# Seven block products of the last layer in another order, with other places for their operands and sums

## The chip, the cores and the metric

The kernel runs on one core of one Trainium2 chip. The metric is device time in microseconds. The kernel before takes 352.95 us (median of 3 runs, 352.54 to 353.83).

Engines are named as in the profile: PE (TensorE, matmuls), ACT (ScalarE), DVE (VectorE), POOL (GpSimdE), SP (SyncE, which issues the DMAs). PE writes into PSUM, which has eight banks here; ACT and DVE read the banks out. Each engine runs its instructions in the order of the program and waits where an operand is not there yet, so everything behind a waiting instruction waits too.

## The reference

Local attention over 4 batches, 8 heads and 576 positions, then a soft mixture of 8 experts, then a gated layer. Only the last layer matters here:

```
# x: 2304 tokens x 512, w_in: 512 x 2048, w_out: 2048 x 512, float32
h = x @ w_in
g = h * (1.0 / (1.0 + np.exp(-h)))      # SiLU
return g @ w_out
```

## The kernel before

**What is computed where.** The mixture's 32 slot outputs times `w_in` are kept as `astk` (tile `rv_astk`), and the mixture's weights of all tokens as `ct`, so a block of h is one matmul. The layer's second product `g @ w_out` is done in two ways. The first 768 tokens go through plain products: for each of 16 slices f of the hidden size, operations `h0.f` (matmul), `si0.f` and `gh0.f` (ACT, SiLU in float32 and rounded), `gl0.f` (DVE, the rounding's rest) and `om0.t.f` (three matmuls of 512 columns for each of six token blocks t). `oe0.t` reads the six sums out of the banks.

The other 1536 tokens are done in two rounds c = 0, 1 of 768 tokens, and here the product is cut into 2 x 2 blocks and done with seven block products in place of eight (Strassen's scheme in Winograd's form). The four activation blocks are A, B, C and E (two halves of the tokens, even and odd slices f), each of eight tiles of 128 x 384. Their operations:

- `ch` is the matmul for one tile into bank 6 or 7 in turn, `cs` the SiLU that ACT writes from it to the block's place (L1051). A `ch` needs the `cs` of two tiles earlier to have freed its bank.
- `sx` are sums of blocks on DVE (L1013, or L1016 where two tiles don't lie side by side): B := A - B, D := C - B, A := A + D, D := E - D. Before, D has a place of its own, `x`, the tile that held the plain part's activations.
- `sh` (ACT, L1068) rounds two tiles of a block for one product into a ring of three (`rs_sth`), and `sl` (DVE, L1070) writes the rest (`rt_stl`).
- `pp` is PE's part: twelve matmuls of 384 columns for two tiles; a product has 48 of them. The weights are plain blocks (tiles `ws`) or sums of weight blocks (`t2.*`, `t34.*`, and halves of `ws`), made by `ts` (sums, DVE L715, L717, L719), `th` (rounded, ACT L723) and `tl` (rest, DVE L728).
- `pe` reads banks out: copies on ACT (L1093), adds on DVE (L1097, L1100). `do` stores a piece of the output.

**Places.** SBUF places are reused under other names: place `w15` holds the last weights in float32 (`wt3`), which `ts`, `th` and `tl` of the weight slices 6 and 7 read, and then block E (`raww15`). `w7` holds `wt2`, then the last sums `t34.3`. A new tile in a place can be written when the last reader of the old one is done; the table `FREE` and the lists `place` tell the planner which operations these are.

**What sets the order.** `list_schedule` walks a table of estimated costs, dependencies and priorities, and fixes each engine's order ahead of the launch. What it is not told of it can't plan around: the wait is then there on the chip all the same, and everything behind it in that engine's order stands.

Of the kernel before, what the change touches and what calls it, by code (L numbers as in the profile page):

```python
# [32 lines left out]
def fused_kernel(ctx: ExitStack, tc: tile.TileContext, a: dict):  # L33
# [784 lines left out]
    for f in (0, 1, *range(2, 16, 2)):  # L818
        i = f // 2
# [5 lines left out]
    for i in range(8):  # L825
# [5 lines left out]
                 3: [["cvi3.0"], [f"t{x}{j}.{k}" for j in (2 * (i // 2) - 2, 2 * (i // 2) - 1) for k in (1, 3) for x in "hl"]][i > 1],  # L831
# [59 lines left out]
    def ost(i):  # L891
        return (hsb, lgf, vz, ccf)[i][:, 0:512] if i < 4 else rawt("x")[:, 2048 + 512 * (i - 4):2560 + 512 * (i - 4)]
# [139 lines left out]
    for c in range(NC):  # L1032
        prev = c - 1
        todo = [(b, i) for b in "ABCE" for i in range(8)]
        for b, i in todo:
# [3 lines left out]
            x = f"{c}.{'ABCDE'.index(b)}.{i}"  # L1039
# [3 lines left out]
            if b == "E":  # L1043
                d = ([f"{q}{c}.2.{i//2-2}" for q in ("sh", "sl")] + [f"sx{c}.4.{i//2-2}"] if i >= 4 else
                     [f"{q}{prev}.2.{i//2+2}" for q in ("sh", "sl")] + [f"sx{prev}.4.{i//2+2}"] if c else FREE["w15"])
            elif c:
# [394 lines left out]
```

## Time and profile before

| | before |
|---|---|
| median of 3 runs | 352.95 us |
| the profiled execution | 352.64 us |
| its span, first to last instruction | 350.5 us |
| PE busy | 333.1 us, 95% |
| DVE busy | 264.9 us, 76% |
| ACT busy | 217.8 us, 62% |
| from the last DVE add's start to the end of the span | 3.7 us |

The times in the trace are microseconds from the start of the span. The seven products of round 0 begin at 214.3, and from there on PE has only these products and their `ch` matmuls left, with a few of the plain part in between. The last DVE add starts at 346.77. A row of the timeline gives start, duration, engine, line, operation, tiles, count, and in brackets the engine's idle time before it with what ended it. Matmuls overlap: one of 384 columns lasts 0.33 from start to end, but the next starts 0.17 later.

### The profile page before, as it was taken

To read this page: it belongs to the slowest core of one execution; us is meant where nothing else is said; L and a number is where in the kernel's file an instruction comes from. 1 tells how busy PE (TensorE), PEld (TensorE's weight loads), DVE (VectorE), ACT (ScalarE), POOL (GpSimd) and SP (SyncE) were. 2 spreads that over 40 slices of the span, in tenths; PEclk is the share of its full clock that TensorE was granted. 3 is DMA by queue.
4 is the path that set the end of the run, shared out by engine and by line. 5 is a ranking of instruction groups with operands and counts; after the bars stand their busy time and mean duration, and the time that the engine had idled before them with its cause. 6 is when DMAs were issued, how large, how long until landed. Compare 5 with 4: busy or idle time off the path is not lost.

```text
span 350.5 us, 8136 instructions
## 1 busy us (share of the span) xinstructions
PE 333.1 (95%) x3200; PEld 270.9 (77%) x3211; DVE 264.9 (76%) x478; ACT 217.8 (62%) x623; POOL 74.4 (21%) x121
## 2 busy tenths in 40 slices
PE   7999999998999998999999999969999999999995
PEld 3687877876533336778767879949999999999995
DVE  5778778699620389999999999969755689965651
ACT  2699989886240136687584999765545677644430
POOL 6987978575430000000000000000000000000000
PEclk9999999999999999999999999999999999999999
DMA  7999999999999998645560003100101110001111
GB/s 262 403 406 404 409 396 407 415 412 413 421 415 424 410 417 340 243 179 197 185 280 2 0 0 122 60 0 2 45 1 47 45 47 0 0 3 45 47 45 45
DMA packets 17893, 70.03 MB, mean 200 GB/s; under 512 B 1984, under 2 KB 4288, under 8 KB 12096
## 3 DMA queue, kind: packets, MB, share of 16 engines
q1 hardware_dynamic: 17856, 69.53, 50.3%
q8 instruction: 25, 0.41, 0.5%
q14 instruction: 12, 0.10, 0.1%
HBM read 64.80 MB, written 4.72 MB: 198 GB/s over the span
## 4 chain that ended last, share of the span: by engine, by line
PE 53%; DVE 20%; ACT 10%; DMA 8%; issue 4%; POOL 3%; SPq 1%; ACTq 0%; POOLq 0%; DVEq 0%
PE ps L86 50%; DMA w_wi<-in_w_in 3%; DMA w_wo<-in_w_out 3%; PE ps L312 2%; ACT rt_px L232 2%; DVE x_gz L876 2%; ACT rv_astk L774 2%; DVE rt_stl L1070 2%; DMA rs_raw<-in_v 2%; DVE w_wif L634 1%; POOL rt_px L249 1%; DVE w_wif L632 1%; ACT rt_gtm L867 1%; DVE w_ws L693 1%; DVE w_wt L632 1%
## 5 line engine op out<-in xcount | busy, mean ns | idle before, releaser
L1068 ACT CAST rs_sth<-w_raww 128x768 fp32r<-128x768 f32 (+1 forms) x44 | 34.3, 779 | 34.5 <-PE ps L86 31.6
L1070 DVE TENSOR_TENSOR rt_stl<-w_raww,rs_sth 128x768 fp32r<-128x768 f32 (+1 forms) x44 | 38.6, 882 | 20.3 <-ACT rs_sth L1068 20.3
L86 PE MATMUL ps<-w_ws,x_gz 128*128 128x512 f32 x216 | 53.2, 393 | 0.0
L86 PE MATMUL ps<-rs_sth,w_ws 128*128 128x384 f32 x192 | 51.7, 334 | 0.0
L232 ACT ACTIVATE rt_px<-ps,spaced 128x64 f32<-128x64 f32 x144 | 43.7, 334 | 10.3 <-DVE spaced L228 9.4
L86 PEld LDWEIGHTS ps<-w_ws,x_gz 128*128 128x128 f32 x216 | 40.0, 188 | 8.2 <-DVE x_gz L876 0.7
L86 PEld LDWEIGHTS ps<-rs_sth,w_ws 128*128 128x128 f32 x192 | 34.9, 188 | 0.0
L1051 ACT ACTIVATE w_raww<-ps 128x384 f32<-128x384 f32 x64 | 28.8, 491 | 8.0 <-DVE ra_t2.1_2528 L728 3.3
L86 PE MATMUL ps<-ct_ct,rv_astk 128*128 128x384 f32 x96 | 27.5, 350 | 5.5 <-ACT w_raww L1051 2.4
L232 ACT ACTIVATION_READ_ACCUMULATOR rt_px<-ps,spaced 128x1 f32 x144 | 32.5, 226 | 0.0
L86 PE MATMUL ps<-rt_stl,w_ws 128*128 128x384 f32 x96 | 32.1, 334 | 0.0
L86 PEld LDWEIGHTS ps<-ct_ct,rv_astk 128*128 128x128 f32 x96 | 17.1, 188 | 11.1 <-ACT x_gz L873 4.5
L1070 DVE TENSOR_TENSOR rt_stl<-x_rawx,rs_sth 128x768 fp32r<-128x768 f32 x16 | 15.3, 956 | 11.6 <-ACT rs_sth L1068 11.6
L249 POOL TENSOR_TENSOR rt_px<-rt_px,stats 128x576 f32<-128x576 f32 (+2 forms) x17 | 18.6, 1092 | 8.3 <-DVE stats L245 2.3
L1068 ACT CAST rs_sth<-x_rawx 128x768 fp32r<-128x768 f32 x16 | 13.4, 836 | 9.3 <-PE ps L86 9.1
L86 PEld LDWEIGHTS ps<-rt_stl,w_ws 128*128 128x128 f32 x96 | 18.0, 188 | 0.0
L867 ACT ACTIVATE rt_gtm<-ps 128x768 f32<-128x768 f32 (+1 forms) x17 | 13.2, 775 | 5.3 <-PE ps L86 4.0
L876 DVE TENSOR_TENSOR x_gz<-rt_gtm,x_gz 128x768 fp32r<-128x768 f32 (+1 forms) x17 | 15.4, 906 | 0.5 <-ACT x_gz L873 0.2
L86 PEld LDWEIGHTS ps<-ra_a,rv_v 128*64 128x64 f32 x320 | 13.1, 137 | 2.8 <-DVE ra_a L263 1.1
L86 PE MATMUL ps<-ra_a,rv_v 128*64 128x96 f32 (+2 forms) x320 | 14.6, 241 | 0.5 <-DVE ra_a L263 0.3
L86 PE MATMUL ps<-rb_a,rv_v 128*64 128x96 f32 (+2 forms) x320 | 14.5, 241 | 0.1
L86 PEld LDWEIGHTS ps<-rb_a,rv_v 128*64 128x64 f32 x320 | 13.1, 137 | 1.9 <-issue 1.1
(293 smaller groups left out, 757.1 us busy)
## 6 DMA issues: line engine op xcount, KB each, us to landing
w_wi<-in_w_in SPq DMA_DIRECT2D x7, 1024.0 KB, 7.7
rs_wo<-in_w_out SPq DMA_DIRECT2D x4, 1024.0 KB, 5.8
rk_k<-in_k SPq DMA_DIRECT2D x12, 288.0 KB, 7.7
w_wo<-in_w_out SPq DMA_DIRECT2D x3, 1024.0 KB, 4.8
rs_raw<-in_v SPq DMA_DIRECT2D x9, 288.0 KB, 8.8
rs_raw<-in_q SPq DMA_DIRECT2D x8, 288.0 KB, 6.7
w_more<-in_q SPq DMA_DIRECT2D x8, 288.0 KB, 10.0
w_more<-in_v SPq DMA_DIRECT2D x6, 288.0 KB, 8.2
```

The source lines that it names most:

```text
L86: pe.matmul(out, lhsT=lhsT, rhs=rhs, start=start, stop=stop, skip_group_check=True)
L232: act.activation(out=preg(n)[:, j, :], in_=sj(n, j), func=ACTF.Exp, scale=D ** -0.5, bias=nmx[:, r, j // 3, j % 3:j % 3 + 1], accum_out=su ...
L249: pool.tensor_tensor(out=p, in0=p, in1=rinv[:, n % 2, j0:j1].rearrange("p (j o) -> p j o", o=1).to_broadcast([128, j1 - j0, 64]), op=ALU.mult)
L312: pe.transpose(ps[0:m, c:c + 128], x[:, 128 * t:128 * t + m], ident)
L632: dve.scalar_tensor_tensor(out=out, in0=hi, scalar=0xC0000000, in1=out, op0=ALU.bitwise_and, op1=ALU.bitwise_or)
L634: dve.scalar_tensor_tensor(out=out, in0=lo, scalar=29, in1=out, op0=ALU.logical_shift_right, op1=ALU.bitwise_or)
L774: act.copy(out=asl(f)[32 * r:32 * r + 32], in_=(aqh if r < 2 else aql)[rows])
L867: act.activation(out=cols(gt(f), ss), in_=hbs(ss), func=ACTF.Silu)
L876: dve.tensor_tensor(out=gsl(gbuf(f, 1), ss), in0=gsl(gt(f), ss), in1=gsl(gbuf(f, 0), ss), op=ALU.subtract)
L1051: op(f"cs{x}", "ACT", .42, [f"ch{x}", *d], lambda c=c, b=b, i=i, s=s: act.activation(out=at(c, b, i), in_=bank[6 + s][:, 0:TW], func=ACTF. ...
L1068: op(f"sh{x}", "ACT", cost(c, PRODS[p][0], j, .42, .74), [*src, old, "cvo14" if o < 0 else None], lambda c=c, p=p, j=j: both(c, p, j, 0, l ...
L1070: lambda c=c, p=p, j=j: both(c, p, j, 1, lambda x, h, l: dve.tensor_tensor(out=l, in0=x, in1=h, op=ALU.subtract)))
```

## The change

- **Order of the products** (table `PRODS` and `SEQ`). Before: A, D = C - B, E, B, A, C, D in the order of the table. Now the products are run in the order A, E, C (all plain), then C := C - B, A := A + C, B := A - B and E := E - C.
- **Places.** There is no block D: sums overwrite C and E. `ROOMS` and `ROOM` deal blocks A, E, C, B of round 0 to the places w8 and w12, w11 and w10, w13 (and ends of four others), and `x`. Block B therefore waits for the plain part's last matmul. Place w15 holds only a bank's copy, V.
- **Banks and read-outs.** The first product of a bank pair starts it, and later ones add to it or start it anew. The read-outs are nine steps instead of seven, with eight more ACT copies in all.
- **Dependencies told to the planner.** `th{i}.3` and place w15 now also name the parts `.2` of `tl`.
- **The last product.** Its last two weight slices run for bank 5 first and then for bank 4.
- One plain read-out (`oe0.4`) goes to the end of place w13.

```diff
-                 3: [["cvi3.0"], [f"t{x}{j}.{k}" for j in (2 * (i // 2) - 2, 2 * (i // 2) - 1) for k in (1, 3) for x in "hl"]][i > 1],
+                 3: [["cvi3.0"], [f"t{x}{j}.{k}" for j in (2 * (i // 2) - 2, 2 * (i // 2) - 1) for k in (1, 2, 3) for x in "hl"]][i > 1],
...
-            "w15": [f"tl{i}.{k}" for i in (6, 7) for k in (1, 3)]}
...
+            "w15": [f"tl{i}.{k}" for i in (6, 7) for k in (1, 2, 3)]}
+    ROOMS = ([(p, n) for p in ("w8", "w12") for n in range(4)], [(p, n) for p in ("w11", "w10") for n in range(4)],
+             [("w13", n) for n in range(4)] + [(p, 4) for p in ("w8", "w12", "w11", "w10")], [("x", n) for n in range(8)])
+    ROOM = ("AECB", "EBAC")
...
-    PRODS = (("A", 0, 0), ("D", 1, 2), ("E", 0, 5), ("B", 1, 3), ("A", 2, 1), ("C", 1, 4), ("D", 2, 6))
+    PRODS = (("A", 0, 0), ("C", 0, 2), ("E", 1, 5), ("B", 0, 3), ("A", 1, 1), ("C", 2, 4), ("E", 2, 6))
+    SEQ = (0, 2, 5, 1, 4, 3, 6)
...
+        end = (c, p) == (NC - 1, SEQ[-1]) and i > 5
+        for x, m in ((6, i - 6), (7, i - 6)) if end else ((i, 0), (i, 1)):
...
+            op(f"sx{c}.3.{j}", "DVE", cost(c, "AB", j, .476, .88), r("A") + r("B"), lambda c=c, j=j: csum(c, "B", "A", "B", ALU.subtract, j))
+            op(f"sx{c}.2.{j}", "DVE", cost(c, "CB", j, .476, .88), [f"sx{c}.3.{j}", *r("C"), *st(5)], lambda c=c, j=j: csum(c, "C", "C", "B", ALU.subtract, j))
+            op(f"sx{c}.1.{j}", "DVE", cost(c, "AC", j, .476, .88), [f"sx{c}.2.{j}", *st(0)], lambda c=c, j=j: csum(c, "A", "C", "A", ALU.add, j))
+            op(f"sx{c}.4.{j}", "DVE", cost(c, "EC", j, .476, .88), [f"sx{c}.2.{j}", *r("E"), *st(2)], lambda c=c, j=j: csum(c, "E", "E", "C", ALU.subtract, j))
...
+        X, Y, Z = range(3)
+        for k, p, b, o in ((0, 0, (X,), "T"), (2, 2, (Y, "T"), "T"), (5, 5, (Z,), "V"), (1, 1, (X,), "U"), (4, 4, (Y, "U"), "U"), (8, 4, (Y,), "W"), (3, 3, (X, "V"), "V"), (9, 3, (X, "W"), "W"), (6, 6, (Z, "U"), "U")):
```

In the order of the instructions, three places show what moved.

ACT, where block E's first SiLUs stand. Before, E is `w15_raww15`, written from `ps_81` (PSUM) behind the two casts of the last weight sums `t34.3`, which read `wt3`:

```order
L1051 ACTIVATE w11_raww11_2605<-ps_81 128x384
L723 CAST w7_t34.3_2725<-w15_wt3_2324 128x512
L1051 ACTIVATE w10_raww10_2642<-ps_81 128x384
L723 CAST w7_t34.3_2725<-w15_wt3_2324 128x512
L1093 COPY vz_65<-ps_81 128x384
L1093 COPY cc_68<-ps_81 128x384
L1051 ACTIVATE w15_raww15_2752<-ps_81 128x384 x2
L1068 CAST rs_sth_2546<-x_rawx_2676 128x768
```

Now E is `w11_raww11` and `w10_raww10`, and the same casts stand among E's SiLUs:

```order
L1037 ACTIVATE w11_raww11_2601<-ps_81 128x384 x2
L723 CAST ra_t2.1_2526<-w7_wt2_2189 128x256
L723 CAST ra_t2.1_2526<-w15_wt3_2324 128x256
L1052 CAST rs_sth_2545<-w11_raww11_2601 128x768
L1037 ACTIVATE w10_raww10_2652<-ps_81 128x384 x2
L723 CAST w7_t34.3_2662<-w15_wt3_2324 128x512 x2
L1052 CAST rs_sth_2545<-w11_raww11_2601 128x768
L1037 ACTIVATE w10_raww10_2652<-ps_81 128x384 x2
```

E has left place w15, and no SiLU of a block stands behind the last reader of `wt3` any more.

DVE, around the last weight parts (L728). Before, the sums D (`x_rawx`, L1013 and L1016) stand ahead of the last one, which reads `wt3`, and the casts' rests (`rt_stl`) behind it:

```order
L1070 TENSOR_TENSOR rt_stl_2557<-x_rawx_2676,rs_sth_2546 128x768
L719 TENSOR_TENSOR w15_wt3_2324<-w15_wt3_2324 128x256
L728 TENSOR_TENSOR ra_t2.1_2528<-w7_wt2_2189,ra_t2.1_2528 128x256
L728 TENSOR_TENSOR w7_t34.3_2725<-w15_wt3_2324,w7_t34.3_2725 128x512 x2
L728 TENSOR_TENSOR w4_ws6_2363<-w15_wt3_2324,w4_ws6_2363 128x256
L728 TENSOR_TENSOR w5_ws7_2439<-w15_wt3_2324,w5_ws7_2439 128x256
L728 TENSOR_TENSOR ra_t2.1_2528<-w15_wt3_2324,ra_t2.1_2528 128x256
L1016 TENSOR_TENSOR x_rawx_2676<-w8_raww8_2538,w10_raww10_2642 128x384
L1016 TENSOR_TENSOR x_rawx_2676<-w12_raww12_2573,w10_raww10_2642 128x384
L1016 TENSOR_TENSOR x_rawx_2676<-w11_raww11_2605,w10_raww10_2642 128x384
L1016 TENSOR_TENSOR x_rawx_2676<-w10_raww10_2642 128x384
L728 TENSOR_TENSOR ra_t2.1_2528<-w15_wt3_2324,ra_t2.1_2528 128x256
```

Now all weight parts are through before the first sum (L1001), and the sums begin behind `oe0.5` (L928):

```order
L728 TENSOR_TENSOR ra_t2.1_2526<-w15_wt3_2324,ra_t2.1_2526 128x256
L728 TENSOR_TENSOR w4_ws6_2363<-w15_wt3_2324,w4_ws6_2363 128x256
L728 TENSOR_TENSOR w5_ws7_2439<-w15_wt3_2324,w5_ws7_2439 128x256
L1054 TENSOR_TENSOR rt_stl_2555<-w10_raww10_2652,rs_sth_2545 128x768 x2
L1054 TENSOR_TENSOR rt_stl_2555<-w13_raww13_2694,rs_sth_2545 128x768 x2
L928 COPY x_rawx_2781<-ps_81 128x512
L1001 TENSOR_TENSOR x_rawx_2781<-w8_raww8_2536,x_rawx_2781 128x768
L1001 TENSOR_TENSOR w13_raww13_2694<-w13_raww13_2694,x_rawx_2781 128x768
```

Eight block sums that stood among the weight parts have moved behind them.

PE, around the plain part's last three matmuls, `om0.5.15` (`w5_ws7,x_gz`). Before, they stand between two steps of the first product:

```order
L86 MATMUL ps_81<-ct_ct_1667,rv_astk_1933 128x384 x2
L86 MATMUL ps_81<-w5_ws7_2439,x_gz_1940 128x512 x3
L86 MATMUL ps_81<-ct_ct_1667,rv_astk_1933 128x384
L86 MATMUL ps_81<-rs_sth_2546,w2_ws4_2251 128x384
L86 MATMUL ps_81<-rt_stl_2557,w2_ws4_2251 128x384
```

Now they stand ahead of the last step of the second product, and the `ch` of two tiles of B (`ct_ct,rv_astk`) behind that step:

```order
L86 MATMUL ps_81<-w5_ws7_2439,x_gz_1940 128x512 x3
L86 MATMUL ps_81<-rs_sth_2545,w5_ws7_2439 128x384
L86 MATMUL ps_81<-rt_stl_2555,w5_ws7_2439 128x384
L86 MATMUL ps_81<-rs_sth_2545,w5_ws7_2439 128x384 x2
L86 MATMUL ps_81<-rt_stl_2555,w5_ws7_2439 128x384
L86 MATMUL ps_81<-rs_sth_2545,w5_ws7_2439 128x384
L86 MATMUL ps_81<-ct_ct_1667,rv_astk_1933 128x384 x2
```

The plain part's end has moved back by more than a whole product, and place `x`, now block B's, comes free that much later.

## Rows read from the trace of the kernel before

**Rows 1.** The page: busy time of PE, and its granted clock by slices.

```profile
PE 333.1 (95%) x3200; PEld 270.9 (77%) x3211; DVE 264.9 (76%) x478; ACT 217.8 (62%) x623; POOL 74.4 (21%) x121
...
PEclk9999999999999999999999999999999999999999
```

**Rows 2.** Windows: stretch, busy us (count) of PE, PEld, DVE, ACT, POOL, clock, DMA.

```profile
207.59:226.53 18.94, 18.94 (x100) 17.52 (x100) 18.91 (x32) 18.10 (x40) 0.00 (x0) 1.00 0.22 84
226.53:241.14 14.61, 11.37 (x58) 9.79 (x58) 11.89 (x20) 7.91 (x17) 0.00 (x0) 1.00 0.00 0
241.14:346.73 105.59, 105.59 (x609) 105.27 (x608) 71.34 (x93) 54.65 (x90) 0.00 (x0) 1.00 0.08 27
```

**Rows 3.** Timeline of PE from 227 to 237, where it waits.

```profile
227.74 0.34 PE L86 MATMUL ps<-ct_ct,rv_astk 128*128 128x384 f32 x1
229.00 0.44 PE L86 MATMUL ps<-ct_ct,rv_astk 128*128 128x384 f32 x1 [0.91 <-ACT w_raww L1051]
...
232.22 0.34 PE L86 MATMUL ps<-rs_sth,w_t2.0_1877 128*128 128x384 f32 x1
234.05 0.82 PE L86 MATMUL ps<-ct_ct,rv_astk 128*128 128x384 f32 x2 [1.49 <-ACT w_raww L1051]
235.15 0.44 PE L86 MATMUL ps<-rs_sth,ra_t2.1_2528 128*128 128x384 f32 x1 [0.28 <-ACT rs_sth L1068]
236.15 0.44 PE L86 MATMUL ps<-rt_stl,ra_t2.1_2528 128*128 128x384 f32 x1 [0.55 <-DVE rt_stl L1070]
```

**Rows 4.** Timeline of ACT in the same stretch.

```profile
227.94 0.62 ACT L723 CAST w_t34.3_2725<-w_wt 128x512 fp32r<-128x512 f32 x1 [1.34 <-DVE ra_t2.1_2528 L728]
228.46 0.48 ACT L1051 ACTIVATE w_raww<-ps 128x384 f32<-128x384 f32 x1
...
229.35 0.48 ACT L1093 COPY vz<-ps 128x384 f32<-128x384 f32 x1
...
233.51 0.87 ACT L1051 ACTIVATE w_raww<-ps 128x384 f32<-128x384 f32 x2 [3.29 <-DVE ra_t2.1_2528 L728]
```

**Rows 5.** Timeline of DVE from 217 to 235.

```profile
217.01 1.82 DVE L1013 TENSOR_TENSOR w_raww<-w_raww,w_raww 128x768 f32<-128x768 f32 x2
...
222.30 0.68 DVE L928 COPY x_rawx<-ps 128x512 f32<-128x512 f32 x1
...
227.43 0.41 DVE L728 TENSOR_TENSOR ra_t2.1_2528<-w_wt,ra_t2.1_2528 128x256 fp32r<-128x256 f32 x1
...
231.10 1.49 DVE L1016 TENSOR_TENSOR x_rawx<-w_raww,w_raww 128x384 f32<-128x384 f32 x3
...
232.98 0.42 DVE L728 TENSOR_TENSOR ra_t2.1_2528<-w_wt,ra_t2.1_2528 128x256 fp32r<-128x256 f32 x1
235.13 0.96 DVE L1070 TENSOR_TENSOR rt_stl<-x_rawx,rs_sth 128x768 fp32r<-128x768 f32 x1 [1.74 <-ACT rs_sth L1068]
```

**Rows 6.** Timeline of PE and of ACT around 207, where the plain part's last SiLU ends.

```profile
200.24 4.26 PE L86 MATMUL ps<-w_ws,x_gz 128*128 128x512 f32 x18
204.34 0.51 PE L86 MATMUL ps<-ct_ct,rv_astk 128*128 128x384 f32 x2
204.68 2.22 PE L86 MATMUL ps<-w_ws,x_gz 128*128 128x512 f32 x9
207.14 0.61 PE L86 MATMUL ps<-ct_ct,rv_astk 128*128 128x384 f32 x2 [0.24 <-ACT x_gz L873]
...
205.27 0.41 ACT L723 CAST w_ws<-w_wt 128x256 fp32r<-128x256 f32 x1
205.58 0.81 ACT L867 ACTIVATE rt_gtm<-ps 128x768 f32<-128x768 f32 x1
```

**Rows 7.** Timeline of the last matmul and the last two adds.

```profile
346.24 0.56 DVE L1100 TENSOR_TENSOR hsb<-ps,hsb 128x384 f32<-128x384 f32 x1 [3.89 <-PE ps L86]
346.39 0.34 PE L86 MATMUL ps<-rs_sth,w_ws 128*128 128x384 f32 x1
346.77 0.56 DVE L1100 TENSOR_TENSOR lg<-ps,lg 128x384 f32<-128x384 f32 x1
```

More of the change, by code (lines that the diff above doesn't have):

```diff
@@ L1033, in fused_kernel @@
         prev = c - 1
-        todo = [(b, i) for b in "ABCE" for i in range(8)]
+        todo = [(b, i) for b in "AECB" for i in range(8)]
         for b, i in todo:
@@ L1042, in fused_kernel @@
             hist.append(f"ch{x}")
[L1043 to L1046, printed above, removed]
-                p = {"A": 3, "B": 4, "C": 5}[b]
-                d = [f"{q}{prev}.{p}.{i//2}" for q in ("sh", "sl")]
-            else:
-                d = FREE[home[b, i][0]]
+            if c:
+                p, more = {"A": (1, (1, 4)), "E": (4, ()), "C": (3, ()), "B": (6, ())}[b]
+                d = [f"{q}{prev}.{p}.{i//2}" for q in ("sh", "sl")] + [f"sx{prev}.{k}.{i//2}" for k in more]
+            else:
+                o, n = place(c, b, i)
+                d = FREE[o] + (["do5"] if o == "x" and n > 6 else [])
@@ new lines, in fused_kernel @@
+                op(f"pp{c}.{p}.{i}", "PE", 6 * .172, d, lambda c=c, p=p, i=i: pmm(c, p, i))
+        X, Y, Z = range(3)
+        for k, p, b, o in ((0, 0, (X,), "T"), (2, 2, (Y, "T"), "T"), (5, 5, (Z,), "V"), (1, 1, (X,), "U"), (4, 4, (Y, "U"), "U"), (8, 4, (Y,), "W"), (3, 3, (X, "V"), "V"), (9, 3, (X, "W"), "W"), (6, 6, (Z, "U"), "U")):
+            for m in range(2):
+                last_ = (c, p) == (NC - 1, SEQ[-1])
+                d = [f"pp{c}.{p}.{6 if last_ and m == 0 else 7}", *{2: [f"pe{c}.0.{m}"], 4: [f"pe{c}.1.{m}"], 8: [f"do{c}.2.{m}"], 3: [f"pe{c}.5.{m}"], 9: [f"pe{c}.8.{m}"], 6: [f"pe{c}.4.{m}"]}.get(k, [])]
+                if c:
+                    d += {0: [f"do{prev}.9.{m}"], 5: [f"do{prev}.3.{m}"], 1: [f"do{prev}.6.{m}"]}.get(k, [])
+                else:
+                    d += {0: [f"do{2+m}"], 5: FREE["w15"], 1: [f"do{m}"]}.get(k, [])
+                src = lambda y, m=m, c=c: at(c, y, m) if isinstance(y, str) else bank[BK[y][m]][:, 0:TW]
+                x = f"{c}.{k}.{m}"
+                if len(b) == 1:
+                    op(f"pe{x}", "ACT", .42, d, lambda c=c, b=b, o=o, m=m, src=src: act.copy(out=at(c, o, m), in_=src(b[0])))
+                else:
+                    op(f"pe{x}", "DVE", .476, d, lambda c=c, b=b, o=o, m=m, src=src: dve.tensor_tensor(out=at(c, o, m), in0=src(b[0]), in1=src(b[1]), op=ALU.add))
+                PEB[f"pe{x}"] = {BK[y][m] for y in b if not isinstance(y, str)}
+                if k in (2, 3, 9, 6):
+                    op(f"do{x}", "SP", .4, [f"pe{x}"], lambda c=c, o=o, m=m: sp.dma_start(out=outs(c, o, m), in_=at(c, o, m)))
@@ L1210, in banks @@
             return {6 + CHB["ch" + n[2:]]}
-        if kind in ("pp", "pe"):
-            return {pbank(i[1], m) for m in ((0, 1) if kind == "pp" else (i[2],))}
+        if kind == "pp":
+            return {pbank(i[1], m) for m in range(2)}
+        if kind == "pe":
+            return PEB[n]
         if kind in ("om", "on", "oe"):
```

110 lines of the change are left out of this document (37 added, 73 removed).

## The prediction

> **What bounds the kernel now.** I read the page first: PE is busy 95% of the span and its clock is granted in full in every slice [rows 1], so the question is where PE is not fed. Windows over the end answer it [rows 2]. From 207.59 to 226.53 and from 241.14 to 346.73 PE is busy all the time. Only between them, from 226.53 to 241.14, is it busy 11.37 of 14.61 us. The long last stretch gives the price of one matmul of 384 columns: 105.59 us over 609 is 0.1734 us. What ends the waits in the middle is read from the three timelines, PE first, then the engine that it names, then the one that this names [rows 3 to 5].
>
> The first wait: the `ch` at 229.00 needs bank 7, which the `cs` at 228.46 frees. That `cs` stands on ACT behind a cast of `t34.3` that waited 1.34 us for DVE's part at 227.43, the last reader of `wt2` in place w7. The second: the `ch` pair at 234.05 needs the first two SiLUs of block E, and these waited 3.29 us, until DVE had read `wt3` out of place w15 for the last time (232.98, 0.42 long). DVE came so late because eight block sums (217.01: two in 1.82) stand ahead of its weight parts. The rest follows from the second: cast and rest for the next step come late (235.15, 236.15). So the stall is a chain of PE behind ACT behind DVE, over a reused place.
>
> **The change part by part.**
>
> *The stall in the second product goes.* The stretch holds the product's 48 matmuls and nine `ch`: 57 x 0.1734 = 9.88 us. It took 14.61, so 4.73 us are lost. Start to start, less the matmuls between, that is 1.09 up to 229.00, 1.66 up to 234.05, 0.75 up to 235.15, 0.83 up to 236.15, and 0.40 in small steps behind [rows 3]. In the new order E lies in w11 and w10, which were free long before. ACT's casts of `t34.3` come while PE has plain products to run, and all weight parts are on DVE ahead of the first sum. What was waited for, w15, is now written first by the copy V, after the third product. The wait for `wt3` therefore has more than 8 us of cover (a product is 48 x 0.1734 = 8.32 us). Gain: 4.73.
>
> *The short wait at 207 goes.* Matmuls of 512 columns come every (204.34 - 200.24) / 18 = 0.228 us, so the nine from 204.68 are through at 206.73, but the next `ch` starts at 207.14: 0.41 us are lost behind the last plain SiLU [rows 6]. That SiLU started at 205.58 behind a cast at 205.27. The order now puts this cast behind it, and its own matmuls end at 204.85. It can start at up to 0.6 earlier, and 0.4 is enough. Gain: 0 to 0.41. I take 0.41, since only the cast stood between.
>
> *The end.* The last product now finishes bank 5 six matmuls before bank 4. Before, the first add already started at 346.24, ahead of the last matmul, and the second at 346.77, which is 0.04 after that matmul's end (346.39 + 0.34) [rows 7]. At most 0.04 is to be had; I take none.
>
> *Eight more copies on ACT.* 8 x 0.48 = 3.8 us [rows 4] beside an ACT that is busy 54.65 of 105.59 us [rows 2]: nothing on the path. Without that cover each would cost 0.48. The second copy of a bank stands ahead of a cast for PE. Its bank isn't written again for a product or more, and the ring holds 3 x 2.08 us of matmuls.
>
> [...] Before, the two banks of a product are read by one engine at a time; now DVE's adds and ACT's copies read the same pair Y. No row of before shows such a pair. [...] The order has ACT take Y's second bank first, and no semaphore stands between them. [...]
>
> *What is late next.* Three places, each by counting from 206.73, where PE now runs on.
> (a) Block B goes to place `x`, which is free when `om0.5.15` has run. By the order 30 matmuls of 512 and 116 of 384 columns lie before that: 206.73 + 6.83 + 20.11 = 233.7. PE then has six matmuls (to 234.7) before it needs bank 6 again. ACT's SiLU can start about 233.9; one takes 0.48 and two 0.87 [rows 4]. With 0.05 for each handover (the adds started 0.04 behind their matmuls [rows 7]) the two `ch` are ready at 234.5 and 234.85, and PE comes at 234.7 and 234.9. The margins are 0.2 and about 0. Price: 0 to 0.3.
> (b) The fourth product needs the first sums. DVE starts `oe0.5` at 233.9. Up to the first rest of that product it has that copy (0.68), five sums and one rest of 768 columns (0.96 each, as at 235.13) and two rests in halves (1.1 each, from the 0.55 of an add of 384 columns [rows 7]): 8.6 us, or about 7.6 with the overlap that "two in 1.82" shows [rows 5]. So it is through at 241.5 to 242.5. PE comes at 235.1 + 52 x 0.1734 = 244.1. Cover: 1.6 to 2.6 us.
> (c) Up to the last rest of product B, DVE has 16 sums, 14 rests, four adds and the copy: about 29 us with overlap, 33 without. That is 263 to 267. PE comes at 244.1 + 138 x 0.1734 = 268. Cover: 1 to 5 us.
>
> I take 0.15 for (a), the middle of its bounds, and nothing for (b) and (c).
>
> **Sum.** 4.73 + 0.41 - 0.15 = 5.0 us. The profiled execution took 352.64 (span 350.5 and 2.14 around it), which gives 347.6. The median of the runs, 352.95, lies 0.31 higher, which would give 347.9. I put down 347.7. All else that PE does after 207 is the same number of matmuls.
>
> **Rivals.**
>
> *The sums come late (349.3).* All 16 sums of a round now stand in one row on DVE beside the casts' rests, and each rest waits for a cast. If DVE meets two waits like the one of 1.74 us [rows 5] before the fourth product, 3.5 us against a cover of 1.6 to 2.6 leave 0.9 to 1.9 us on the path, 348.6 to 349.6. For it: DVE's row is long and B is late. Against: the rest that waited 1.74 stood behind the blocked SiLUs, which are gone.
>
> *The wait only moves (352).* The new `x` takes w15's part: B's SiLUs wait for the plain part's end as E's did for `wt3`. If each of the four pairs of B's `ch` came 1.1 us late, 4.4 us would be given back: 347.6 + 4.4 = 352.0. For it: the margin at (a) is about nothing. Against: between pairs PE has 12 matmuls, 2.08 us, and ACT has two SiLUs (0.87) and a cast in halves (under 1), so a first delay isn't repeated.
>
> *Slower: DVE becomes the bound of a round (360).* From 226.53 to 241.14 DVE was busy 81% of the time [rows 2]. If it did its 33 us at that share, it would need 40.7 us where PE has 268.0 - 233.7 = 34.3. The excess of 6.4 would come in both rounds: 347.5 + 12.8 = 360. It decides from a share under 89% in the two rounds: 33 / 0.89 = 37.1, 2.8 too much in each, 353.2. Against: before, DVE did the same sums in round 1 with 71.34 us busy of 105.59, and PE didn't wait once [rows 2].
>
> **How the numbers follow.** Forecast 0.72, sums late 0.14, wait moves 0.09, slower 0.05. The low end is both gains whole with the 0.04 of the end, 347.5, less the 0.4 by which the fastest run lies under the median: 347.0. The high end takes in the rival of late sums up to its own 349.6 and the offset of the median: 350.0. That leaves out about 2 in 10. A measurement of this kernel tells about 0.5%, 1.8 us, from no change. Faster by more than that are the first two cases, 0.86; within it, 0.09; slower, 0.05.
>
> **What would show it.** In the changed kernel's windows PE should be busy throughout from 204 to its last matmul, at 342 instead of 346.7. No SiLU of a block should wait for a DVE part of the weights. Around 233.7 ACT should wait about 1 us for PE ahead of B's first SiLU, and PE at most 0.3 behind it. DVE should run nearly closed from there for 30 us with PE not waiting. The last add should still start about 0.05 behind the last matmul. I am wrong if PE waits at the first matmul of the fourth product, or at the `ch` of B by more than 1 us, or if the clock falls in the closed stretch, which it didn't in 105 us before [rows 2].

## The result, and the profile after

The changed kernel takes 347.27 us (median of 4 runs, 347.13 to 347.34), beside 352.75 us for the kernel before (median of 4 runs, 351.73 to 353.83). The ratio is 0.9844, with a 95% interval of 0.9814 to 0.9874. The forecast was 347.7 us, in a range of 347.0 to 350.0. The profiled execution took 347.13 us.

The page of the changed kernel gives the span and the engines' busy time, to set beside [rows 1]:

```profile
span 345.0 us, 8170 instructions
...
PE 333.1 (97%) x3211; PEld 271.5 (79%) x3211; DVE 265.1 (77%) x488; ACT 221.0 (64%) x635; POOL 74.6 (22%) x121
...
PEclk9999999999999999999999999999999999999999
```

PE is busy for the same 333.1 us in a span that is 5.5 us shorter. The windows that answer to [rows 2], and a fourth over the new row of sums (columns: stretch, busy us and count of PE, PEld, DVE, ACT, POOL, clock, DMA):

```profile
207.58:226.53 18.95, 18.82 (x102) 17.53 (x101) 17.43 (x34) 18.18 (x39) 0.00 (x0) 1.00 0.15 57
226.53:241.14 14.61, 14.61 (x84) 14.30 (x83) 10.00 (x14) 10.29 (x22) 0.00 (x0) 1.00 0.10 37
241.14:341.23 100.09, 100.09 (x578) 99.77 (x576) 74.28 (x106) 54.65 (x96) 0.00 (x0) 1.00 0.08 28
233.77:263.13 29.36, 29.36 (x171) 29.32 (x170) 28.82 (x44) 16.97 (x32) 0.00 (x0) 1.00 0.08 29
```

The stretch that was busy for 11.37 of 14.61 us is now full. Only the first window has a hole, 0.13 us of idle. The timelines of PE and ACT around 207 show both the wait that went and this new one (columns as in [rows 6]):

```profile
204.01 2.23 PE L86 MATMUL ps<-w_ws,x_gz 128*128 128x512 f32 x9
206.08 0.51 PE L86 MATMUL ps<-ct_ct,rv_astk 128*128 128x384 f32 x2
...
208.15 0.84 PE L86 MATMUL ps<-w_ws,x_gz 128*128 128x512 f32 x3
209.13 0.44 PE L86 MATMUL ps<-ct_ct,rv_astk 128*128 128x384 f32 x1
209.41 0.39 PE L86 MATMUL ps<-w_ws,x_gz 128*128 128x512 f32 x1
...
205.69 0.40 ACT L723 CAST ra_t2.1_2526<-w_wt 128x256 fp32r<-128x256 f32 x1
205.98 0.41 ACT L723 CAST w_ws<-w_wt 128x256 fp32r<-128x256 f32 x1
206.64 0.41 ACT L723 CAST w_ws<-w_wt 128x256 fp32r<-128x256 f32 x1 [0.24 <-DVE w_wt L715]
206.95 0.86 ACT L1037 ACTIVATE w_raww<-ps 128x384 f32<-128x384 f32 x2
...
208.59 0.87 ACT L1037 ACTIVATE w_raww<-ps 128x384 f32<-128x384 f32 x2
```

Nine matmuls of 512 columns from 204.01 are through at 206.06, and the `ch` pair follows at 206.08: the 0.41 us of [rows 6] are gone. But the three from 208.15 are through at 208.83, and the next `ch` starts at 209.13. That `ch` waits for a SiLU at 208.59. It is late because of what stands ahead of it on ACT: three weight casts (205.69, 205.98 and 206.64), of which the third waited 0.24 for DVE, and from there on without a gap block A's first two SiLUs, a cast, and this one. The wait costs 0.30, and 0.11 more before the next matmul. Three casts stood ahead of A's first SiLUs before as well (206.98 to 207.58), but none of them waited, and PE had six plain matmuls between its `ch` pairs there, where it now has three.

Around 233.77, where place `x` comes free, and at the first steps of the row of sums, ACT and DVE read:

```profile
233.77 0.88 ACT L1037 ACTIVATE x_rawx<-ps 128x384 f32<-128x384 f32 x2 [1.17 <-PE ps L86]
...
233.77 0.69 DVE L928 COPY x_rawx<-ps 128x512 f32<-128x512 f32 x1 [0.94 <-PE ps L86]
234.68 0.96 DVE L1001 TENSOR_TENSOR x_rawx<-w_raww,x_rawx 128x768 f32<-128x768 f32 x1 [0.21 <-ACT x_rawx L1037]
235.67 0.96 DVE L1001 TENSOR_TENSOR w_raww<-w_raww,x_rawx 128x768 f32<-128x768 f32 x1
...
241.03 0.95 DVE L1054 TENSOR_TENSOR rt_stl<-w_raww,rs_sth 128x768 fp32r<-128x768 f32 x1
...
243.70 0.95 DVE L1054 TENSOR_TENSOR rt_stl<-w_raww,rs_sth 128x768 fp32r<-128x768 f32 x1
...
263.84 0.96 DVE L1054 TENSOR_TENSOR rt_stl<-x_rawx,rs_sth 128x768 fp32r<-128x768 f32 x1 [0.70 <-ACT rs_sth L1052]
```

PE waits at none of these places. It starts the fourth product at 244.00, and the rest for its first step is through at 241.03 + 0.95 = 241.98: 2.0 us of cover. The rest of the second step is through at 244.65, and PE comes at 246.08: 1.4 us. The last row is the last rest of product B, through at 264.80; PE comes for it at 267.92.

**From which row the two executions are compared.** Each trace counts from its own first instruction, and the early part, which the change leaves alone, isn't equally long in all executions. The last row of it that I use is this one on DVE, first of the kernel before, then of the changed one:

```profile
154.65 1.22 DVE L693 TENSOR_TENSOR w_ws<-w_wt,w_ws 128x1024 fp32r<-128x1024 f32 x1
```

```profile
153.94 1.22 DVE L693 TENSOR_TENSOR w_ws<-w_wt,w_ws 128x1024 fp32r<-128x1024 f32 x1
```

So 0.71 of the 5.50 us by which PE's last matmul starts earlier (346.39 before [rows 7], 340.89 after) were there ahead of the change. The change's own part is 4.79 us. All runs below are compared in this way: the start of PE's last matmul, less the start of this row.

| kernel | row at 154 | last matmul | between | over the changed kernel |
|---|---|---|---|---|
| before | 154.65 | 346.39 | 191.74 | +4.79 |
| changed | 153.94 | 340.89 | 186.95 | 0 |
| changed, again (e5) | 153.75 | 340.68 | 186.93 | -0.02 |
| before, both places told (e1) | 153.89 | 342.89 | 189.00 | +2.05 |
| before, w15 told (e2) | 154.05 | 344.12 | 190.07 | +3.12 |
| changed, sums third (e3) | 154.34 | 343.63 | 189.29 | +2.34 |
| changed, casts late (e4) | 154.18 | 341.05 | 186.87 | -0.08 |
| changed, E in w15 (e6) | 154.24 | 342.29 | 188.05 | +1.10 |
| changed, copy five times (e7) | 153.95 | 344.51 | 190.56 | +3.61 |
| changed, copies twice (e8) | 154.86 | 341.99 | 187.13 | +0.18 |
| changed, rest four times (e9) | 154.54 | 343.01 | 188.47 | +1.52 |
| changed, E in w15, told (e10) | 154.57 | 341.66 | 187.09 | +0.14 |
| changed, old end (e11) | 154.94 | 341.87 | 186.93 | -0.02 |
| changed, casts and copy (e12) | 154.22 | 340.81 | 186.59 | -0.36 |

Two executions of the changed kernel agree to 0.02 in this measure, while the row at 154 lies between 153.75 and 154.94. Where a text speaks of what PE "loses", it is start to start, less the matmuls between at 0.1734 us (384 columns) or 0.228 (512).

### The profile page after: what moved, and what is told of

The parts are those of the page before. It is cut to its first block, busy times and chain, and to the rows that moved or that the text cites. A ratio compares the mean times of both kernels' runs of the same rounds, so it can differ in the third digit from the quotient of the medians.

```text
span 345.0 us, 8170 instructions
## 1 busy us (share of the span) xinstructions
PE 333.1 (97%) x3211; PEld 271.5 (79%) x3211; DVE 265.1 (77%) x488; ACT 221.0 (64%) x635; POOL 74.6 (22%) x121
## 4 chain that ended last, share of the span: by engine, by line
PE 72%; DVE 15%; ACT 8%; issue 3%; DMA 1%; POOL 0%; ACTq 0%; DVEq 0%
PE ps L86 68%; PE ps L312 3%; ACT rv_astk L774 2%; DVE x_gz L876 2%; DVE w_wif L634 2%; DVE w_wif L632 2%; DVE w_wt L632 1%; DVE w_wt L634 1%; ACT rt_gtm L867 1%; DVE w_ws L693 1%; ACT w_ws L687 1%; ACT x_gz L873 1%; DMA rs_raw<-in_q 1%; DVE w_wt L630 1%; DVE w_wif L630 1%
## 5 line engine op out<-in xcount | busy, mean ns | idle before, releaser
L1054 DVE TENSOR_TENSOR rt_stl<-w_raww,rs_sth 128x768 fp32r<-128x768 f32 (+1 forms) x52 | 42.7, 833 | 25.2 <-ACT rs_sth L1052 25.1
L1052 ACT CAST rs_sth<-w_raww 128x768 fp32r<-128x768 f32 (+1 forms) x52 | 38.3, 739 | 31.9 <-PE ps L86 26.5
L86 PE MATMUL ps<-ct_ct,rv_astk 128*128 128x384 f32 x96 | 26.3, 346 | 2.2 <-ACT x_gz L873 1.2
L1037 ACT ACTIVATE w_raww<-ps 128x384 f32<-128x384 f32 x48 | 21.1, 488 | 0.1
L1052 ACT CAST rs_sth<-x_rawx 128x768 fp32r<-128x768 f32 x12 | 10.1, 838 | 11.8 <-PE ps L86 11.2
L227 DVE TENSOR_REDUCE stats<-ps 128x9 f32<-128x576 f32 x16 | 11.8, 738 | 3.4 <-PE ps L86 1.8
```

The costliest lines, as they stand in the source:

```text
L86: pe.matmul(out, lhsT=lhsT, rhs=rhs, start=start, stop=stop, skip_group_check=True)
L227: dve.tensor_reduce(out=mxs[:, n % 2], in_=ps[:, c:c + 64 * NJ].rearrange("p (j c) -> p j c", c=64), axis=AXX, op=ALU.max)
L1037: op(f"cs{x}", "ACT", .42, [f"ch{x}", *d], lambda c=c, b=b, i=i, s=s: act.activation(out=at(c, b, i), in_=bank[6 + s][:, 0:TW], func=ACTF. ...
L1052: op(f"sh{x}", "ACT", cost(c, PRODS[p][0], j, .42, .74), [*src, old, "cvo14" if o < 0 else None], lambda c=c, p=p, j=j: both(c, p, j, 0, l ...
L1054: lambda c=c, p=p, j=j: both(c, p, j, 1, lambda x, h, l: dve.tensor_tensor(out=l, in0=x, in1=h, op=ALU.subtract)))
```

## The experiments

Theory: PE waited for ACT, and ACT for DVE, over two reused places that the planner had not been told of in full; moving E out of w15 and the sums behind the plain products removes it. Rivals: telling the planner alone would do it (e1); or the order of the products alone. The second was run only in part: e6 takes back the telling of w15 and the new place of two of E's eight tiles, and no run has the new order with both places untold.

**Before, with the two dependencies told (e1).** Places, products and sums stay as before.

```diff
-... for k in (1, 3) for x in "hl"]][i > 1],
+... for k in (1, 2, 3) for x in "hl"]][i > 1],
...
-            "w15": [f"tl{i}.{k}" for i in (6, 7) for k in (1, 3)]}
+            "w15": [f"tl{i}.{k}" for i in (6, 7) for k in (1, 2, 3)]}
```

> The kernel before, with one thing of the change: the planner is told that place w15 and the last t34 sums also wait for the parts .2 of tl (both dependency lines). Order of the products, places and read-outs stay. My theory (a chain over reused places, and sums that are needed right behind the first product): the 3.29 us that ACT waited ahead of block E's first SiLUs go, because DVE is now made to read wt3 earlier, but the second product still needs D = C - B from a DVE that is full of weight parts, so PE still loses 1 to 2.5 of the 4.73 us there. Time 2 to 3.5 us under the kernel before. Rival (what the planner was not told is all of it): the loss goes wholly, 4.5 to 5 us under the kernel before, as the changed kernel.

Measured: 349.64 us (4 runs, 349.17 to 349.97), beside 353.36 for before (7 runs); ratio 0.9897, 0.9865 to 0.9929. In the trace 2.74 of the 4.79 us are gained, 2.05 are left. The timelines of DVE, ACT and PE where the rest is lost:

```profile
228.06 1.29 DVE L728 TENSOR_TENSOR w_t34.3_2733<-w_wt,w_t34.3_2733 128x512 fp32r<-128x512 f32 x2
229.27 1.49 DVE L1016 TENSOR_TENSOR x_rawx<-w_raww,w_raww 128x384 f32<-128x384 f32 x3
...
230.37 1.79 ACT L1068 CAST rs_sth<-x_rawx 128x768 fp32r<-128x768 f32 x2 [2.29 <-DVE x_rawx L1016]
...
231.26 0.44 PE L86 MATMUL ps<-rs_sth,ra_t2.1_2528 128*128 128x384 f32 x1 [0.60 <-ACT rs_sth L1068]
232.48 0.45 PE L86 MATMUL ps<-rt_stl,ra_t2.1_2528 128*128 128x384 f32 x1 [0.78 <-DVE rt_stl L1070]
```

No SiLU waits for a weight part now. Instead the last sums of D come behind the weight parts on DVE, ACT's cast waits 2.29 us for them, and PE, in the second product already, loses 0.77 at the first of the two rows and 1.05 at the second. Telling the planner is worth a little more than half; the other part hangs on a product of sums being second.

**Before, with only w15 told (e2).** The second of the two lines above.

> The kernel before with the told dependency for place w15 alone. My theory: the two waits are separate places; the one at 229 (1.09 us, behind the cast of t34.3 that waits for wt2) stays, of the 3.24 us behind place w15 one to two go. Time 1 to 2.2 us under the kernel before, and more than e1_told by about 1. Rival (w15 alone is the cause): 3 us or more go and the time is that of e1_told.

Measured: 350.79 us (4 runs), ratio 0.9926, 0.9898 to 0.9954; 3.12 us over the changed kernel, so w15 alone gives 1.67. The wait over w7 is still there, as in [rows 3]:

```profile
228.39 0.44 PE L86 MATMUL ps<-ct_ct,rv_astk 128*128 128x384 f32 x1 [0.89 <-ACT w_raww L1051]
```

It loses 1.06 ahead of this row, and 2.74 - 1.67 = 1.07 is what e1 gains on top. The two places add up.

**Changed, with the product of C - B third (e3).** The new places and banks, and both dependencies told; only the order of the products differs.

```diff
-    SEQ = (0, 2, 5, 1, 4, 3, 6)
+    SEQ = (0, 5, 1, 2, 4, 3, 6)
```

> The changed kernel with the product of C - B run third instead of fourth, ahead of the plain product of E (order A, C, C - B, E, A + C, B, E - C). Places, read-outs and told dependencies as in the changed kernel. If the plain products ahead are what covers the sums (cover 1.6 to 2.6 us with three of them, 8.3 us a product), PE waits again: 1 to 6 us lost, at the first step of C - B or at the matmuls for block B. Rival (the places alone did it): no wait, within 0.5 us of the changed kernel.

Measured: 349.91 us (4 runs), ratio 0.9898, 0.987 to 0.9926; 2.34 us over the changed kernel. PE is again busy throughout from 226 to 241; it waits in the other products (PE, then ACT):

```profile
254.67 0.45 PE L86 MATMUL ps<-ct_ct,rv_astk 128*128 128x384 f32 x1 [0.96 <-ACT w_raww L1037]
...
318.77 0.41 PE L86 MATMUL ps<-rs_sth,rk_ws 128*128 128x384 f32 x1 [0.40 <-DVE vz L1087]
...
253.40 0.83 ACT L1052 CAST rs_sth<-w_raww 128x768 fp32r<-128x768 f32 x1 [1.19 <-PE ps L86]
254.13 0.87 ACT L1037 ACTIVATE w_raww<-ps 128x384 f32<-128x384 f32 x2
```

The order with all plain products first is worth 2.34 us here, near the 2.05 that e1 left. But PE does not wait for a sum in this run, which the expectation had. It loses 1.54 around 254 to a SiLU that stands behind a cast which waited for the ring, and 0.66 at 318 to a read-out that stands behind a rest on DVE. So the size agrees with the theory and the mechanism is another; that the sums would come late in this order is not shown.

**Changed, with E's first two tiles back in w15, untold (e6).** The first two rooms of E's list go to w15 in place of w11, and `tl{i}.2` is left out of w15's list again.

```diff
-            "w15": [f"tl{i}.{k}" for i in (6, 7) for k in (1, 2, 3)]}
-    ROOMS = (..., [(p, n) for p in ("w11", "w10") for n in range(4)],
+            "w15": [f"tl{i}.{k}" for i in (6, 7) for k in (1, 3)]}
+    ROOMS = (..., [("w15", 2), ("w15", 3)] + [(p, n) for p in ("w11", "w10") for n in range(4)][2:],
```

> The changed kernel with block E's first two tiles of round 0 put back into place w15, and the last weight parts left out of the planner's list again; order of the products, sums and banks stay new. Theory (a block in the place of the last weights puts its SiLUs behind VectorE's weight parts): the SiLUs of E's first tiles wait on ACT for the last reader of wt3, and TensorE waits 0.5 to 1.5 us between 214 and 230, so 0.5 to 1.5 us more than the changed kernel. Rival (with the plain products ahead the place matters no more): within 0.3 us of the changed kernel.

Measured: 348.38 us (4 runs) beside 347.49 for the changed kernel on the same chip; 1.10 over it in the trace. The chain is there again, DVE, ACT, PE:

```profile
221.53 0.75 DVE L728 TENSOR_TENSOR ra_t2.1_2528<-w_wt,ra_t2.1_2528 128x256 fp32r<-128x256 f32 x2
...
222.36 0.87 ACT L1037 ACTIVATE w_raww<-ps 128x384 f32<-128x384 f32 x2 [3.26 <-issue]
...
222.91 0.82 PE L86 MATMUL ps<-ct_ct,rv_astk 128*128 128x384 f32 x2 [0.28 <-ACT w_raww L1037]
```

The last readers of `wt3` end at 222.28, ACT stood idle for 3.26 us and starts at 222.36, and PE loses 0.46, 0.31 and 0.29 at and behind this place. The bracket says "issue", since the profile shows no releaser; that it is DVE is read from the times.

**The same, told (e10).** `tl{i}.2` back in w15's list, E still in w15.

> As the kernel with E's first two tiles in place w15, but with the last weight parts told to the planner. Untold, it lost 0.92 us more on TensorE than the changed kernel. Theory (what costs is the untold wait): within 0.3 us of the changed kernel, since the planner now puts other work ahead. Rival (the place itself costs, told or not): 0.7 to 1.0 more than the changed kernel, as untold.

Measured: 347.87 us (4 runs, 347.41 to 347.96), 0.14 over the changed kernel in the trace. The wait on ACT is still there, as E's first SiLUs show:

```profile
222.08 0.88 ACT L1037 ACTIVATE w_raww<-ps 128x384 f32<-128x384 f32 x2 [2.66 <-issue]
```

In e6 they start 0.08 behind the last reader of `wt3` (222.36 behind 222.28); here they stand behind 2.66 us of idle time on ACT. But the order now has PE at other matmuls meanwhile, and PE loses nothing here. So it is not the place that costs, nor the wait as such, but that the order was made without it.

**Changed, with the copy `oe0.5` five times (e7).**

```diff
-            op(f"oe0.{t}", "DVE", .6, d, lambda t=t: dve.tensor_copy(ost(t), obank(t)))
+            op(f"oe0.{t}", "DVE", .6, d, lambda t=t: [dve.tensor_copy(ost(t), obank(t)) for _ in range(5 if t == 5 else 1)])
```

> The changed kernel with the copy of the plain part's last sum done five times in place of once: four more copies of 0.60 us each, back to back, just ahead of VectorE's row of block sums, 2.4 us in all, with no other instruction moved. It measures the cover of the row. In the trace of the changed kernel the rests of products 4 to 6 are through 1.4 to 2.1 us before TensorE's matmuls for them. Theory (cover 1.4, and one row without slack): TensorE waits 2.4 - 1.4 = 1.0 us, 0.6 to 1.4, once, at one of the steps of the fourth to sixth product, so 348.3 where the changed kernel has 347.3. Rival (cover of 2 to 5 us, since VectorE catches up at its waits for the ring): at most 0.3 us.

Measured: 349.62 us (4 runs, 349.25 to 350.74), 3.61 over the changed kernel in the trace: both theories miss. The copy holds a bank that the third product writes, and PE waited there, not at the sums (timeline of PE, then windows with the columns above):

```profile
237.43 0.44 PE L86 MATMUL ps<-rs_sth,w_t34.0_2055 128*128 128x384 f32 x1 [1.75 <-DVE x_rawx L928]
...
239.23 0.52 PE L86 MATMUL ps<-rs_sth,w_t34.0_2055 128*128 128x384 f32 x1
239.55 0.84 PE L86 MATMUL ps<-ct_ct,rv_astk 128*128 128x384 f32 x2
```

```profile
235.69:237.43 1.74, 0.00 (x0) 0.00 (x0) 1.67 (x4) 0.55 (x2) 0.00 (x0) 1.00 0.00 0
237.43:238.42 0.99, 0.99 (x5) 0.99 (x6) 0.96 (x2) 0.10 (x1) 0.00 (x0) 1.00 0.19 70
238.42:242.24 3.82, 3.82 (x15) 3.82 (x14) 3.82 (x7) 1.69 (x4) 0.00 (x0) 0.55 0.15 55
242.24:250.00 7.76, 7.76 (x46) 7.76 (x46) 7.26 (x12) 4.75 (x10) 0.00 (x0) 1.00 0.00 1
```

The wait itself cost 1.91 + 0.12 us. On top, one microsecond behind it, the granted clock fell to about half for 3.8 us, and the matmuls came every 0.32 us; that cost the other 1.6. Without the fall it would by this estimate have been 2.03 over the changed kernel. The three timed runs with a mean clock of 0.999 or more took 349.25 to 349.79 us, the profiled one, with 0.994, 350.74. The five copies came every 0.73 us in place of the 0.60 that were expected; this is an estimate from the 3.68 us between the end of the plain part's last matmul (233.75) and PE's start at 237.43, less 0.69 for the last copy and 0.04 for each of the two handovers [rows 7], over four. The run tells nothing of the row of sums, so the next one pushes it at another place.

**Changed, with the first rest of the fourth product four times (e9).**

```diff
-... lambda c=c, p=p, j=j: both(c, p, j, 1, lambda x, h, l: dve.tensor_tensor(...)))
+... lambda c=c, p=p, j=j: [both(c, p, j, 1, lambda x, h, l: dve.tensor_tensor(...)) for _ in range(4 if (c, p, j) == (0, 1, 0) else 1)])
```

> The changed kernel with the first rest of the fourth product done four times in place of once: three more operations of 0.87 us, 2.6 us in all, within VectorE's row of sums, and nothing else moved. The fives copies of the run before this stood on a bank that TensorE needed, so they told of that bank, not of the row. Theory (the row of sums has a cover of 2.0, 1.4, 1.6 and 1.9 us at the four steps of the fourth product, as read from the changed kernel's trace): TensorE waits 0.6 us at the first step and another 0.6 at the second, 1.2 in all (1.0 to 1.5), and not again. Rival (VectorE gains time at its waits for the ring, the cover being 2.6 or more): below 0.3. A fall of the clock behind a wait would come on top and is to be read from the matmul's spacing (0.32 in place of 0.17 us).

Measured: 349.16 us (4 runs, 348.79 to 349.24), 1.52 over the changed kernel in the trace, just above the expected 1.0 to 1.5. DVE, then PE:

```profile
241.59 3.93 DVE L1054 TENSOR_TENSOR rt_stl<-w_raww,rs_sth 128x768 fp32r<-128x768 f32 x4
245.44 1.02 DVE L1004 TENSOR_TENSOR w_raww<-w_raww,x_rawx 128x384 f32<-128x384 f32 x2
...
245.58 0.45 PE L86 MATMUL ps<-rt_stl,w_t2.0_1877 128*128 128x384 f32 x1 [0.68 <-DVE rt_stl L1054]
...
248.25 0.44 PE L86 MATMUL ps<-rt_stl,w_t2.0_1877 128*128 128x384 f32 x1 [0.31 <-DVE rt_stl L1054]
```

Four rests into the same piece of the ring took longer than I had put down: a single one hands over after 0.87 us (241.03 to 241.90 in the changed kernel), here the next operation starts 3.85 after the first, so the row is pushed by 2.98 us, not 2.6. PE loses 0.95 at the first step (0.84 and 0.11) and 0.59 at the second (0.47 and 0.12), and nothing behind. That makes a cover of 2.98 - 0.95 = 2.03 at the first step and 2.98 - 1.54 = 1.44 at the second, the 2.0 and 1.4 that the changed kernel's rows show.

**Changed, with each copy of ACT done twice (e8).**

```diff
-... lambda c=c, b=b, o=o, m=m, src=src: act.copy(out=at(c, o, m), in_=src(b[0])))
+... lambda c=c, b=b, o=o, m=m, src=src: [act.copy(out=at(c, o, m), in_=src(b[0])) for _ in range(2)])
```

> The changed kernel with each of ScalarE's copies out of the banks done twice, sixteen more of up to 0.48 us each (0.38 back to back). Theory (ScalarE is covered behind 214): no more than 0.1 us. Rival (the copies stand ahead of casts that TensorE waits for): 16 x 0.4 = 6.4 us at most, and 1.5 or more if one pair in four delays a cast.

Measured: 347.89 us (4 runs, 347.33 to 348.22) beside 347.49; 0.18 over the changed kernel in the trace, a little more than the 0.1 expected. PE loses 0.22 behind one `ch` pair at 295.14 and nothing at the other copies. Sixteen more copies cost that little, so the eight that the change added are covered.

**Changed, with the last product ended as before (e11).**

```diff
-        end = (c, p) == (NC - 1, SEQ[-1]) and i > 5
+        end = False
...
-                last_ = (c, p) == (NC - 1, SEQ[-1])
+                last_ = False
```

> The changed kernel with the last product ended as before (both banks in turn for each weight slice). Theory: 0 to 0.05 us more, with the second of the last adds 0.04 behind the last matmul or 0.04 behind the first add's end. Rival (the new end saves an add): 0.5 us more.

Measured: 348.01 us (4 runs); PE's last matmul -0.02 from the changed kernel. The last add of this kernel, and then that of the changed one:

```profile
342.24 0.56 DVE L1087 TENSOR_TENSOR lg<-ps,lg 128x384 f32<-128x384 f32 x1
```

```profile
341.27 0.56 DVE L1087 TENSOR_TENSOR lg<-ps,lg 128x384 f32<-128x384 f32 x1 [0.49 <-PE ps L86]
```

It starts 0.37 after the last matmul's start with the old end (341.87) and 0.38 with the new one (340.89). The new end gives nothing.

**Changed, with three weight casts behind the first SiLUs (e4), and with a read-out told as well (e12).** The wait at 209 stands behind three casts; e4 tells the planner to put these later. e12 adds one more pair.

```diff
+    for x, y in [('th5.1', 'cs0.0.3'), ('th4.1', 'cs0.0.1'), ('th4.2', 'cs0.0.1')]:
+        ops[x][2].append(y)
```

> The changed kernel with three weight casts (th4.1, th4.2, th5.1) told to come behind the first SiLUs of block A. In the changed kernel's trace PE loses 0.41 us at 209, where ACT's SiLUs of A stand behind these casts, one of which waited 0.24 us for DVE. If that is the cause, the 0.41 go: 0.3 to 0.4 us under the changed kernel, and no lost time on PE between 204 and its end. Rival (the wait only moves to the next pair of matmuls, or DVE's later parts are missed): the same time as the changed kernel or up to 0.5 more.

> The changed kernel with three weight casts told to stand behind the first SiLUs, as in the run that moved the wait of 0.41 us at 209 to the first product's second bank (0.30 us at 213), and with VectorE's copy of that bank told ahead of the rest that stood before it. Theory (both waits are one untold order each): both go, and TensorE loses 0.1 to 0.2 between 203 and 245 where the changed kernel loses 0.4 to 0.6; 0.3 to 0.4 us below the changed kernel. Rival (the wait moves again): no gain, within 0.1.

Measured: e4 347.45 us (4 runs), -0.08 against the changed kernel. The wait at 209 is gone, and another is there, at the first product's second bank. PE, then DVE of e4:

```profile
212.90 0.81 PE L86 MATMUL ps<-rs_sth,rk_ws 128*128 128x384 f32 x2
213.55 0.34 PE L86 MATMUL ps<-rt_stl,rk_ws 128*128 128x384 f32 x1
...
211.54 0.95 DVE L1054 TENSOR_TENSOR rt_stl<-w_raww,rs_sth 128x768 fp32r<-128x768 f32 x1
212.53 0.69 DVE L928 COPY lg<-ps 128x512 f32<-128x512 f32 x1
```

Two such matmuls last 0.51 elsewhere, here 0.81: the second goes to the bank that DVE copies out until 213.22. PE loses 0.19 there and 0.11 behind it, so 0.30 of the 0.41 us came back 4 us later, and the expected gain of 0.3 to 0.4 did not come: the rival was right. The planner also spread PE's `ch` matmuls anew in this run, so that the casts alone made the wait at 209 is not shown. With the copy told ahead of the rest (`('sl0.0.1', 'oe0.1')` added to the list), e12 takes 347.03 us (4 runs, 346.87 to 347.53) beside 348.01 and 347.87 for e11 and e10 on the same chip, and lies 0.36 below the changed kernel in the trace. PE is busy for 42.00 of the 42 us from 203 to 245. The planner made a different order from there on, in which that copy in fact starts no earlier (212.91), so the gain is measured, and which of its moves brought it isn't. By the trace it beats both kernels; by medians 0.4 us is too little to tell.

## Why the prediction was right, point by point

- **The stall in the second product, 4.73.** Right in size: the second window is full, and the whole change measures 4.79. The chain over the places was right too, but it was not the whole of it. Telling the planner of the same waits in the old order gave 2.74 (e1). The other 2.05 hangs on what the prediction named only as the reason why DVE was late, eight block sums ahead of the weight parts: with the places told, DVE's order is turned round and the sums come late. Both halves of the change were needed, places (or telling) and order.
- **The short wait at 207, 0.41.** Right that it goes, wrong that nothing takes its place. The planner put the cast behind the last plain SiLU, as the prediction says, and with it ahead of A's first SiLUs; 0.41 us were lost at 209. The step that failed is the search for "what is late next": it began at block B, and did not look at A's first SiLUs, two microseconds behind the removed wait. Term 0.41 measured about 0: counted in the same way, with the second matmul behind each wait, the old one cost 0.52 and the new one 0.41.
- **(a) Block B at `x`, price 0.15.** It measured 0. ACT's SiLUs start at 233.77, the `ch` pair follows at 234.63 without a wait. The count gave 233.7 and 233.9, but 0.71 of earlier start and 0.41 of new wait lie in between, so that the time came out within 0.15 is partly luck.
- **(b) The first sums.** Predicted cover 1.6 to 2.6; 2.03 at the first step by e9. The bound missed the second step, which is tighter, 1.44. The rival of late sums needed 3.5 us of waits on DVE; the row was busy for 28.82 of 29.36, so it had 0.54.
- **(c) The long row on DVE.** Right: the row is closed until 263.13, and the last rest of product B, 0.70 later because of its cast, is through at 264.80, inside the 263 to 267. PE comes for it at 267.92, a cover of 3.1 in the forecast 1 to 5, and does not wait anywhere in the row. The slower rival (a busy share of 81% on DVE) is refuted by the share of 98%.
- **The copies and the end.** Both at 0 as put down (e8, e11). In the profiled execution the two engines never read one bank of the pair Y at once: in round 0 DVE is through with the first bank at 261.78 and ACT starts on it at 261.95; ACT is through with the second at 262.05 and DVE starts on it at 262.58. In round 1 DVE is through with both at 325.31 and ACT starts at 325.37. So no run shows what reading one bank at the same time does.
- **The sum.** 4.73 + 0.41 - 0.15 = 5.0 against 4.73 + 0.41 - 0.41 = 4.73 by these terms, and 4.79 measured. The stall's 4.73 is the bulk of it. 352.64 - 4.79 = 347.85 would have been the profiled time; it was 347.13, since the early part was 0.71 shorter. That part is scatter between executions, as the table's second column shows. The forecast lies 0.4 above the measured median: the terms were 0.2 too large, and the medians differ by 0.7 more than the traces do. That the two errors went against each other is luck.

The medians differ by more than 4.79: 5.5 us in the first comparison and 6.1 in the second (347.49, 5 runs, beside 353.61, 9 runs). One part is the clock of the kernel before, below. Its five executions with a mean clock of 0.999 or more have a median of 352.75, and the nine of the changed kernel one of 347.34: 5.4. The last 0.6 is within the scatter of the early part, and stays open. The changed kernel was run again (e5) to tell whether the change makes the early part shorter: that rival had the medians 5.5 us apart and the row at 154 again 0.7 earlier than in the kernel before, and at 6.1 us and 0.90 it fits better than the theory of 4.8. But e1 and e2, with the products, places and read-outs of the kernel before, have this row at 153.89 and 154.05, and the kernels made from the changed one at 153.75 to 154.94. DVE's and ACT's orders are the same in both kernels up to 194. So the row scatters whichever order follows, and the rival isn't borne out.

## What to carry to other kernels

A dependency that the planner didn't know of was still waited for here, with everything behind it (3.29 us on ACT [rows 4]); look for brackets on ACT or DVE that name an unrelated engine's last reader of a reused place, and tell the planner before moving anything. Then ask again what is late: almost half the loss (2.05 of 4.79 us, e1) remained until the work that needs sums was put behind work that doesn't, and two small waits came back a few microseconds later when they were removed (0.41 us at 209, 0.30 at 213). For a gain of 1%, compare traces from a row that the change leaves alone, and measure a cover by pushing the row, not by the counted slack alone.

## What the runs showed of the hardware

**In one execution the granted clock fell behind a wait of PE.** In the profiled execution of e7 PE was busy for 9.60 of 9.60 us from 226.00 to 235.60, stood for 1.74 us, ran 0.99 us at a granted clock of 1.00, and then 3.82 us at 0.55 in the mean, with matmuls of 384 columns every 0.32 us in place of 0.17; from 242.24 to 250.00 it was at 1.00 again. So the wait of 2.03 us came with another 1.6. The fall came once in this execution (the page has an 8 in one slice and a 9 in the others), behind the 1.74 us without a matmul. Three other executions of the same kernel kept a mean clock of 0.999 or more, so the fall does not come each time, and why it comes is not shown.

**The kernel before had a mean clock below 0.999 in most of its runs.** Of 23 of its executions beside the experiments, five had a mean clock of 0.999 to 1.0 and took 352.37 to 353.15 us, twelve had 0.995 (353.17 to 354.12), and six had 0.988 or 0.99 (354.69 to 355.18). Of the 53 executions of the other kernels, two lay that low (0.994 in e7, 0.995 in e11). The profiled execution of before had a mean clock of 0.999, with a 9 in every slice [rows 1], so no trace shows where the clock fell. That it was behind its stall is the author's argument: from e7, and from e1 and e2, which had 0.997 or more in all eight executions, where five of the seven of before on the same chip had 0.995 or less. e2 differs from before by one told dependency, and it still loses 3.12 us, so it would be the part of the stall over w15 that the falls go with. If so, the change takes away an estimated 1 us more in the mean (353.76 for all 23 beside 352.72 for the five) that the profile of before could not show.

**Three times here, operations on DVE that used what the one just before them used or wrote came about 0.12 us later.** In the changed kernel's row, operations of 768 columns mostly start 0.08 before the end of the one ahead of them, and so follow each other after 0.87 (239.29, 240.16, 241.03, 241.90). The four rests of e9, which write to one piece of the ring, came every 0.99 (3.93 for four, 0.95 of it the last): each starts 0.03 to 0.04 behind the end of the one before. The five copies of e7 came every 0.73, by the estimate above (a single one of the changed kernel at 222.43 takes 0.60 to the next operation), and the second sum of the changed kernel's row, which reads the first, came after 0.99 (234.68, then 235.67). What takes the 0.12 is not shown. In e9 the repeated operation pushed by this larger figure: 2.98 us, where the expectation had 2.6.
